# A split-precision first layer whose rescaling pass is dropped: three recombined passes summed in PSUM, units one by one

## The chip, the cores and the metric

The kernel runs on one core of a Trainium2 chip. The metric is device time in microseconds (us); the kernel before takes 2204.26 us, the median of three runs (2204.12 to 2204.32). The engines are called by the profile's names: PE is TensorE (PEld its weight loads), DVE VectorE, ACT ScalarE, POOL GpSimd, SP SyncE.

## The reference

A causal convolution along the sequence, with softmaxed weights per head, and then a two-layer perceptron with a hardswish between the layers:

```
x: 8 x 4096 x 192      weight: 8 heads x 7 taps
w   = softmax(weight) over the taps
y[b, s, h, :] = sum over k of w[h, k] * x_padded[b, s + k, h, :]   # 6 zeros ahead of the sequence
h   = y (32768 x 192) @ w_in (192 x 2048)
g   = h * clip(h + 3, 0, 6) / 6
out = g @ w_out (2048 x 192)                                     # float32
```

## The kernel before

The 32768 tokens are cut into 32 blocks of 1024. In a block, tokens 0 to 511 have their 192 channels on partitions 0 to 63 (three thirds per partition) and tokens 512 to 1023 on partitions 64 to 127. So a first-layer matmul works on 64 rows and 512 tokens, and two of them, one per half of the partitions, run side by side.

Block 0 is done in a plain way (`out_direct`, L341), while the weights of the others are prepared. Blocks 1 to 31 each call `first_layer` and then `second_layer`, and everything around them is written out by hand: the program's order on each engine is the order of the calls.

**The first layer in three passes.** The product y @ w_in is wanted in full precision but computed in a faster matmul format (`F32R`), whose operands are rounded. So y and w_in are each split. Of y the kernel makes three parts (L1068 to L1085): high p (`high_of`, ACT, L476, a multiplication by `CUT`), low l = y - p (`split_low`, DVE, L1081) and mix (`split_mix`, DVE, L479). Of w_in it makes three once, in the start (`w_parts`, L484). A unit is one of 16 pieces of a block's hidden features: 8 with the halves of the partitions as they lie (`y_own`), then 8 with the halves swapped (`y_other`, made by six DMAs from POOL's queue, L266 and L267). A unit has a slot of two PSUM banks out of four slots, and goes like this:

- `begin(n)`: the HIGH pass and the LOW pass, each three thirds times two halves, six matmuls (L511), into one slot; then both banks are multiplied by 4097 in place, by ACT (L523, 128x1024). For the last unit of a block ACT does one bank (L526) and DVE the other (L527).
- `end(n)`: the MIX pass adds six more matmuls to the rescaled sums; then ACT's `relu` (L302) and DVE's `gate` (L306) make g from the slot, which is free after that.

The order is begin(0), begin(1), then for every n end(n) and begin(n + 2); close to the end of the block begin(15) comes ahead of end(13). Hence the unit's third pass stands behind nine other matmul pairs or so, while ACT rescales. Between the units stand `jobs`: the last sums and stores of the block before (`finish`), and one tap of the convolution of the block after the next (L1058, DVE, 128x1536) after every second unit. POOL makes small sums of g (L603) beside it.

**The second layer.** It is computed by a scheme with seven products of halves of g and w_out in place of eight, partly two levels deep, with four streams of matmuls side by side in column tiles of 32 (L653). `second_layer` writes the streams with a clock of 80 steps; `do(t, fn)` puts the work of the other engines at a time t of that clock, and the events are then issued sorted by time. `level_two` issues one product at the second level and copies its pieces out of PSUM at the clock of the matmuls plus `late_by`. `negative(pair)` (L572 on ACT, then an accumulating DMA from POOL's queue, L569) makes a piece of S3, which product 3 reads at the end. `split_high`, `split_low` and `split_mix` of the next block stand at the times 48.4, 57 and 70. In the last block (`last`) some of it stands in another order, for a shorter end.

Of the kernel before, what the change touches and what calls it, by code (L numbers as in the profile page):

```python
# [8 lines left out]
ALU = mybir.AluOpType  # L9
# [8 lines left out]


CUT = 1.0 - 2.0**-13  # L20
EPS = 2.0**-12
HIGH, LOW, MIX = range(3)


# [1 line left out]
def kernel(  # L26
# [8 lines left out]
    nc = tc.nc  # L35
# [11 lines left out]
    K3 = D // D2  # L47
# [424 lines left out]
    def r32(ap):  # L472
        return ap.bitcast(F32R)

    def high_of(out, x, scale=1.0):
        nc.scalar.mul(r32(out), x, CUT * scale)  # L476

    def from_high(out, high, scale, x, op):
        nc.vector.scalar_tensor_tensor(  # L479
            out=r32(out), in0=high, scalar=scale, in1=x, op0=ALU.mult, op1=op  # L480
        )
# [17 lines left out]
    def first_layer(i, jobs):  # L499

        slots = {}

        def both(n):
            return psum[:, 2 * slots[n] : 2 * slots[n] + 2]

        def mms(n, part, start=False, stop=False):
            group, c = divmod(n, NP)
            for s in range(K3):
                for k in range(2):
                    r = slice(k * D2, (k + 1) * D2)  # L510
                    nc.tensor.matmul(  # L511
                        out=psum[:, 2 * slots[n] + k], lhsT=r32(w_in_parts[part][r, c, s]),
                        rhs=r32(y_other[0][r, part, s] if group else y_own[part][r, s]),
                        start=start and s == 0, stop=stop and s == K3 - 1,
                        skip_group_check=True,
                    )

        def begin(n):
            slots[n] = free_slots.pop(0)
            mms(n, HIGH, start=True)  # L520
            mms(n, LOW)
            if n + 1 < count:
                nc.scalar.mul(both(n), both(n), 4097.0)  # L523
            else:
                lower, upper = (psum[:, 2 * slots[n] + k] for k in range(2))
                nc.scalar.mul(lower, lower, 4097.0)  # L526
                nc.vector.tensor_scalar(  # L527
                    out=upper, in0=upper, scalar1=4097.0, scalar2=None, op0=ALU.mult
                )
# [12 lines left out]
        for job in jobs.get(-1, ()):  # L542
            job()
        for n in range(count):
            if n == count - 3:
                begin(n + 2)
            end(n)
            if n < count - 3:
                begin(n + 2)
            for job in jobs.get(n, ()):  # L550
                job()
            if n < NP and n % 2:
                small_sums(shared, A11, (3, 2, 4), nc.gpsimd, every[n - 1 : n + 1])
            if n == NP - 1:
                sums4[:] = [pools[0].tile([P, NP, N], F32, name="z4", tag="own")]
                nc.sync.dma_start(out=four_parts(sums4[0])[0], in_=four_parts(A22)[2])
                small_sums(sums4[0], A22, (3,), nc.gpsimd, every[:4])
            if n == NP + 1:
                third_sum(0, nc.vector)
                add_pair(0)  # L560
                adding(four_parts(sums4[0])[0], four_parts(A22)[3])
                small_sums(sums4[0], A22, (3,), nc.gpsimd, every[4:])
            if n == NP + 3:
                third_sum(1)
                small_sums(sums4[0], A22, (2,), nc.gpsimd)
                add_pair(1)
# [54 lines left out]
    def second_layer(i, between):  # L621
# [118 lines left out]
        def level_two(n, p, order, j=3):  # L740
# [197 lines left out]
    with tc.manual_schedule():  # L938
# [129 lines left out]
        def split_y():  # L1068
            new_parts()
            high, low, mix = y_own  # L1070
            high_of(high[:], y[:])
            split_low()
            split_mix()

        def split_high():
            new_parts()
            high_of(y_own[HIGH][:], y[:])

        def split_low():
            high, low, mix = y_own  # L1080
# [87 lines left out]
```

## Time and profile before

| what | us |
|---|---|
| median of three runs | 2204.26 |
| the profiled execution | 2203.68 |
| its span (from the first to the last instruction) | 2201.9 |
| PE busy | 2193.5 |
| DVE busy | 1983.1 |
| ACT busy | 1738.8 |
| POOL busy | 1181.4 |
| a first layer on the chain that ended last | 32.97 |
| a second layer on that chain | 34.61 |
| rescaling on ACT (L523, 465 times 1008 ns) | 468.7 |

A row of a group gives line, engine, operation, output and inputs, partitions x elements and how many there were, then busy time in us and mean ns of one, then the engine's idle time just before them and what ended most of it. A row of the timeline gives start, duration and the same names; a note in square brackets is idle time of that engine ahead of the row, with what ended it. Several equal instructions that follow each other stand in one row (x24), whose duration runs from the first start to the last end. A row of the waits gives who waited for whom, the total in us, how often, and the longest. The granted TensorE clock is 0.999 of full speed over the span.

### The profile page before, as it was taken

How to read it: one execution, taken by the hardware profiler on the slowest of the kernel's cores; microseconds unless marked ns; L12 is line 12 of the kernel's file. 1: busy time of each engine (PE TensorE's matmuls, PEld its weight loads, DVE VectorE, ACT ScalarE, POOL GpSimd, SP SyncE). 2: the span in 40 equal slices, each digit the busy share in tenths (PEclk: the TensorE clock that was granted, in tenths of full speed). 3: DMA queues.
4: the chain of work that ended last, by engine and by line, in shares of the span. 5: the costliest groups of instructions: out<-in, count | busy, mean ns of one | idle time of the engine just before them, and what ended most of it. 6: DMA issues, size and time to landing. Idle time of an engine off the chain costs nothing.

```text
span 2201.9 us, 55361 instructions
## 1 busy us (share of the span) xinstructions
PE 2193.5 (100%) x22984; PEld 1564.6 (71%) x22984; DVE 1983.1 (90%) x1983; ACT 1738.8 (79%) x2391; POOL 1181.4 (54%) x1033
## 2 busy tenths in 40 slices
PE   9999999999999999999999999999999999999998
PEld 5477777777777777777777777777777777777776
DVE  8899998999898989989999999999899998999977
ACT  7488787787877878877878778787788887787876
POOL 2456644556544665445655456554456544556544
PEclk9999999999999999999999999999999999999999
DMA  6277778777778777797777887777877778777787
GB/s 158 56 141 142 144 148 154 139 144 145 146 140 159 139 140 143 146 163 131 144 146 146 149 148 141 145 144 144 159 134 141 145 148 155 136 145 143 134 142 121
DMA packets 353308, 313.20 MB, mean 142 GB/s; under 512 B 212480, under 2 KB 265216, under 8 KB 353056
## 3 DMA queue, kind: packets, MB, share of 16 engines
q0 software_dynamic: 114976, 234.46, 59.2%
q1 hardware_dynamic: 236840, 74.93, 16.9%
q8 instruction: 180, 2.95, 0.6%
q14 instruction: 72, 0.59, 0.1%
q10 hardware_dynamic: 1240, 0.27, 0.1%
HBM read 31.72 MB, written 25.17 MB: 26 GB/s over the span
## 4 chain that ended last, share of the span: by engine, by line
PE 99%; DVE 0%; DMA 0%; SPq 0%; ACT 0%; issue 0%; DVEq 0%; ACTq 0%
PE psum L653 49%; PE psum L511 46%; PE psum L296 2%; PE psum L341 2%; DMA x<-in_x_dram 0%; DVE shared L458 0%; SPq L100 0%; DVE shared L464 0%; SPq L133 0%; DVE top L175 0%; PE psum L953 0%; DVE y L255 0%; SPq L89 0%; ACT y L967 0%; ACT scale L186 0%
## 5 line engine op out<-in xcount | busy, mean ns | idle before, releaser
L653 PE MATMUL psum<-g,w_out 128*32 128x512 f32 (+1 forms) x5968 | 824.2, 503 | 0.0
L306 DVE SCALAR_TENSOR_TENSOR g<-g,psum 128x1024 f32<-128x1024 f32 (+1 forms) x528 | 619.2, 1186 | 108.3 <-ACT g L302 107.9
L653 PE MATMUL psum<-s,w_out 128*32 128x512 f32 (+1 forms) x3024 | 712.1, 585 | 0.0
L302 ACT ACTIVATE g<-psum,half 128x1024 f32<-128x1024 f32 (+1 forms) x528 | 565.2, 1087 | 5.9 <-PE psum L511 5.1
L653 PEld LDWEIGHTS psum<-g,w_out 128*32 128x32 f32 x5968 | 382.1, 110 | 221.9 <-issue 112.2
L511 PE MATMUL psum<-y_own,w_in 64*128 64x512 f32 x4464 | 523.3, 389 | 0.0
L511 PE MATMUL psum<-y_other,w_in 64*128 64x512 f32 x4464 | 516.0, 386 | 0.0
L523 ACT ACTIVATE psum<-psum 128x1024 f32<-128x1024 f32 x465 | 468.7, 1008 | 48.3 <-PE psum L511 46.2
L511 PEld LDWEIGHTS psum<-y_own,w_in 64*128 64x128 f32 x4464 | 413.5, 184 | 117.6 <-issue 26.0
L511 PEld LDWEIGHTS psum<-y_other,w_in 64*128 64x128 f32 x4464 | 418.1, 184 | 87.8
L603 POOL TENSOR_TENSOR shared<-g,shared 128x256 f32<-128x256 f32 x248 | 356.9, 1439 | 89.8 <-DVE g L306 58.1
L1058 DVE SCALAR_TENSOR_TENSOR y<-x,c_sb,y 128x1536 f32<-128x1536 f32 x186 | 335.2, 1802 | 1.5 <-ACT y L1056 1.3
L569 POOL DMA_DIRECT2D s<-g x124 | 148.4, 1197 | 293.5 <-ACT s L572 246.7
L653 PE MATMUL psum<-g,w_s 128*32 128x256 f32 x1488 | 284.5, 379 | 0.0
L653 PEld LDWEIGHTS psum<-s,w_out 128*32 128x32 f32 x3024 | 231.8, 110 | 34.5 <-issue 11.2
L569 POOL DMA_DIRECT2D g<-g x124 | 181.7, 1530 | 104.6 <-DVE s L414 104.6
L653 PE MATMUL psum<-z,w_s 128*32 128x256 f32 x992 | 227.7, 379 | 0.0
L653 PE MATMUL psum<-z,w_out 128*32 128x256 f32 x992 | 227.0, 379 | 0.0
L603 POOL TENSOR_TENSOR shared<-g 128x256 f32<-128x256 f32 x124 | 91.6, 739 | 174.1 <-DVE g L306 174.1
L650 ACT COPY psum<-psum 32x512 f32<-32x512 f32 x186 | 82.9, 446 | 116.1 <-PE psum L653 113.2
L458 DVE TENSOR_TENSOR g<-g 128x1024 f32<-128x1024 f32 x124 | 149.4, 1221 | 19.3 <-PE psum L653 17.1
L653 PEld LDWEIGHTS psum<-g,w_s 128*32 128x32 f32 x1488 | 137.8, 110 | 38.1
(115 smaller groups left out, 2870.1 us busy)
## 6 DMA issues: line engine op xcount, KB each, us to landing
y_other<-y_own POOLq DMA_DIRECT2D x180, 384.0 KB, 8.1
g<-g POOLq DMA_DIRECT2D x124, 512.0 KB, 6.1
s<-g POOLq DMA_DIRECT2D x124, 512.0 KB, 6.3
z<-g POOLq DMA_DIRECT2D x62, 512.0 KB, 7.5
out_dram<-shared SPq DMA_DIRECT2D x378, 64.0 KB, 4.3
x<-in_x_dram SPq DMA_DIRECT2D x53, 388.5 KB, 5.7
z<-g SPq DMA_DIRECT2D x31, 512.0 KB, 3.3
stage<-in_moe_w_in_dram SPq DMA_DIRECT2D x16, 192.0 KB, 4.6
```

Source lines behind the costliest of these rows:

```text
L296: nc.tensor.matmul(out=psum[:, b], lhsT=w[r], rhs=src, start=start, stop=stop, skip_group_check=onto,)
L302: nc.scalar.activation(r6, h, ACT.Relu, bias=half[:], scale=1.0 / 6.0)
L306: nc.vector.scalar_tensor_tensor(out=g_, in0=g_, scalar=1.0, in1=h, op0=ALU.min, op1=ALU.mult)
L341: lambda p=p: nc.tensor.matmul(out=bank[j * QS : (j + 1) * QS, tokens], lhsT=w_out[:, p, w, cols], rhs=x[:, p, tokens], start=(first and p ...
L458: nc.vector.tensor_tensor(out=out, in0=x, in1=y, op=op)
L511: nc.tensor.matmul(out=psum[:, 2 * slots[n] + k], lhsT=r32(w_in_parts[part][r, c, s]), rhs=r32(y_other[0][r, part, s] if group else y_own[ ...
L523: nc.scalar.mul(both(n), both(n), 4097.0)
L569: nc.gpsimd.dma_start(out=out, in_=x, accum_op=ALU.add)
L603: engine.tensor_tensor(out=o, in0=p, in1=q, op=op)
L650: streams[3].append((t - 0.5, lambda: fn(*args, **kw)))
L653: nc.tensor.matmul(out=out, lhsT=w, rhs=x, start=start, stop=True, tile_position=(0, j * QS), skip_group_check=True,)
L1058: jobs.append(lambda k=k: nc.vector.scalar_tensor_tensor(out=y[:], in0=x[:, :, k : k + N], scalar=c_sb[:, k : k + 1], in1=y[:], op0=ALU.mu ...
```

## The change

The three products are combined in another way. With y = p + l and w_in = H + L, where p and H are exact in the matmul format, the sum is now

p H + l (H + 4097 L) + (p - 4096 l) L,

in which the terms with 4096 and 4097 leave l L over: p H + l H + 4097 l L + p L - 4096 l L = (p + l)(H + L). Nothing has to be rescaled, so all 18 matmuls of a unit add to one another in PSUM. H is now w_in times 1 + 2^-13 in the rounded format. The parts stand in the order p with H, l with H + 4097 L, p - 4096 l with L, and the third part of y is -4096 l + p in place of p / 4096 - l.

A unit's 18 matmuls now stand together; unit n + 1's come ahead of the relu and gate of unit n. Two events of the last block's second layer are moved: the copy of product 4's second piece from 19.3 to 8.2 clock steps behind its matmuls, and the fourth `negative` from time 52 to 44.3. On the engines' queues this takes out 465 + 31 + 2 passes of ACT (L523, L526, L487) and 31 of DVE (L527) and moves one copy and one negation on ACT in the last block, its DMA with it; the order of POOL's and SP's instructions stays, and DVE's but for the passes taken out.

```diff
-EPS = 2.0**-12
+RAISE = 1.0 + 2.0**-13
...
-    def w_parts(high, low, mix, w):
-        high_of(high, w, EPS)
-        from_high(mix, high, 4097.0, w, ALU.subtract)
-        from_high(low, high, -4096.0, w, ALU.add)
-        nc.scalar.mul(r32(mix), mix, -4096.0)
+    def plus(out, x, scale, y):
+        nc.vector.scalar_tensor_tensor(
+            out=r32(out), in0=x, scalar=scale, in1=y, op0=ALU.mult, op1=ALU.add
+        )
+    def w_parts(high, sum_, low, w):
+        high_of(high, w, RAISE)
+        plus(low, high, -1.0, w)
+        plus(sum_, low, 4097.0, high)
...
-        def begin(n):
-            slots[n] = free_slots.pop(0)
-            mms(n, HIGH, start=True)
-            mms(n, LOW)
-            if n + 1 < count:
-                nc.scalar.mul(both(n), both(n), 4097.0)
-            else:
-                lower, upper = (psum[:, 2 * slots[n] + k] for k in range(2))
-                nc.scalar.mul(lower, lower, 4097.0)
-                nc.vector.tensor_scalar(
-                    out=upper, in0=upper, scalar1=4097.0, scalar2=None, op0=ALU.mult
-                )
         def end(n):
             group, c = divmod(n, NP)
-            mms(n, MIX, stop=True)
             to = g4[:, c, 1:3] if group else g4[:, c, 0::3]
             relu(to, both(n))
             gate(to, both(n))
             free_slots.append(slots[n])
-        begin(0)
-        begin(1)
+        steps = [(part, s) for part in range(3) for s in range(K3)]
+        mms(0)
         for job in jobs.get(-1, ()):
             job()
         for n in range(count):
-            if n == count - 3:
-                begin(n + 2)
+            if n + 1 < count:
+                mms(n + 1)
             end(n)
-            if n < count - 3:
-                begin(n + 2)
...
-                    late_by = {(1, 2): 8.1, (4, 2): 19.3}.get((n, k), 0.02 if n == 4 else 0)
+                    late_by = {(1, 2): 8.1, (4, 2): 8.2 if last else 19.3}.get((n, k), 0.02 if n == 4 else 0)
...
-        for r, t in zip(chunk_pairs, (34.3, 36.3, 42.1, 52)):
+        for r, t in zip(chunk_pairs, (34.3, 36.3, 42.1, 44.3 if last else 52)):
             do(t, negative, r)
...
         def split_mix():
             high, low, mix = y_own
-            from_high(mix[:], high[:], EPS, low[:], ALU.subtract)
+            plus(mix[:], low[:], -4096.0, high[:])
```

More of the change, by code (lines that the diff above doesn't have):

```diff
@@ L473, in r32, with high_of @@
         return ap.bitcast(F32R)
-    def high_of(out, x, scale=1.0):
-        nc.scalar.mul(r32(out), x, CUT * scale)
-    def from_high(out, high, scale, x, op):
+    def high_of(out, x, by):
+        nc.scalar.mul(r32(out), x, by)
+    def plus(out, x, scale, y):
         nc.vector.scalar_tensor_tensor(
-            out=r32(out), in0=high, scalar=scale, in1=x, op0=ALU.mult, op1=op
+            out=r32(out), in0=x, scalar=scale, in1=y, op0=ALU.mult, op1=ALU.add
         )
-    def w_parts(high, low, mix, w):
-        high_of(high, w, EPS)
-        from_high(mix, high, 4097.0, w, ALU.subtract)
-        from_high(low, high, -4096.0, w, ALU.add)
-        nc.scalar.mul(r32(mix), mix, -4096.0)
+    def w_parts(high, sum_, low, w):
+        high_of(high, w, RAISE)
+        plus(low, high, -1.0, w)
+        plus(sum_, low, 4097.0, high)
     free_slots = list(range(4))
@@ L504, in both, with mms @@
             return psum[:, 2 * slots[n] : 2 * slots[n] + 2]
-        def mms(n, part, start=False, stop=False):
+        def mms(n):
+            slots[n] = free_slots.pop(0)
             group, c = divmod(n, NP)
-            for s in range(K3):
+            for part, s in steps:
                 for k in range(2):
@@ L513, in mms @@
                         rhs=r32(y_other[0][r, part, s] if group else y_own[part][r, s]),
-                        start=start and s == 0, stop=stop and s == K3 - 1,
+                        start=(part, s) == steps[0], stop=(part, s) == steps[-1],
                         skip_group_check=True,
                     )
-        def begin(n):
-            slots[n] = free_slots.pop(0)
-            mms(n, HIGH, start=True)
-            mms(n, LOW)
-            if n + 1 < count:
-                nc.scalar.mul(both(n), both(n), 4097.0)
-            else:
-                lower, upper = (psum[:, 2 * slots[n] + k] for k in range(2))
-                nc.scalar.mul(lower, lower, 4097.0)
-                nc.vector.tensor_scalar(
-                    out=upper, in0=upper, scalar1=4097.0, scalar2=None, op0=ALU.mult
-                )
         def end(n):
             group, c = divmod(n, NP)
-            mms(n, MIX, stop=True)
             to = g4[:, c, 1:3] if group else g4[:, c, 0::3]
@@ L1070, in split_y @@
             high, low, mix = y_own
-            high_of(high[:], y[:])
+            high_of(high[:], y[:], CUT)
             split_low()
@@ L1076, in split_high @@
             new_parts()
-            high_of(y_own[HIGH][:], y[:])
+            high_of(y_own[HIGH][:], y[:], CUT)
         def split_low():
```

## The prediction

> **What bounds the kernel now.** I read the page's head first, then the chain that ended last in order of time, then TensorE's own waits, then the timelines of one block (the one whose first layer starts at 978.3 us; the blocks repeat to 0.01 us).
>
> ```profile
> span 2201.9 us, 55361 instructions
> PE 2193.5 (100%) x22984; PEld 1564.6 (71%) x22984; DVE 1983.1 (90%) x1983; ACT 1738.8 (79%) x2391; POOL 1181.4 (54%) x1033
> ```
> ```profile
> 943.79 34.61 PE psum L653 x289
> 978.40 32.97 PE psum L511 x288
> ```
> The chain is TensorE throughout: 31 times a first layer (L511, 288 matmuls, 32.97 us), then a second layer (L653, 34.61 us). The change edits the first layer, so what can be gained is what its 32.97 us hold beyond matmuls. All durations come from one profiled execution. ScalarE looks like the bound there, and a table of busy time by stage, from the third unit on, seems to say so:
>
> ```profile
> 981.40:1009.00 27.60, 27.60 (x246) 22.77 (x246) 25.61 (x20) 27.52 (x27) 19.95 (x17) 1.00 0.67 141
> ```
> Columns: stretch, length, then PE, PEld, DVE, ACT, POOL. ACT is busy 27.52 of 27.60 us, but PE all 27.60. Who waits for whom decides:
>
> ```profile
> PEld psum L511 <- issue: 26.0, 31, 0.8
> PEld psum L511 <- ACT psum L523: 6.8, 30, 0.2
> ```
> TensorE's weight loads wait for the rescaling (L523) once per block, 30 times, 6.8 us in all. That is load idle, not lost time; the matmul rows give the loss. Two matmuls, one per half of the rows, start together; I call them a pair.
>
> ```profile
> L511 PE MATMUL psum<-y_other,w_in 64*128 64x512 f32 x4464 | 516.0, 386 | 0.0
> ```
> ```profile
> 978.33 3.02 PE L511 MATMUL psum<-y_own,w_in 64*128 64x512 f32 x24
> ...
> 980.73 13.64 PE L511 MATMUL psum<-y_own,w_in 64*128 64x512 f32 x118
> 994.21 1.52 PE L511 MATMUL psum<-y_other,w_in 64*128 64x512 f32 x12
> ...
> 996.25 15.12 PE L511 MATMUL psum<-y_other,w_in 64*128 64x512 f32 x132
> ```
> The last row is 66 pairs, so 65 spacings in 15.12 - 0.386 us: 0.2267 us each, and 144 of them are 32.64 us. The 12 pairs from 978.33 take 3.02 - 0.386 - 11 x 0.2267 = 0.14 us too long: the start of the stage. The 59 pairs from 980.73 take 13.64 - 0.386 - 58 x 0.2267 = 0.11 us too long: the wait, at the first unit's third pass. The remaining 0.08 of 32.97 is the hand-over to the second layer.
>
> **The change part by part.**
>
> *The rescaling goes.*
>
> ```profile
> L306 DVE SCALAR_TENSOR_TENSOR g<-g,psum 128x1024 f32<-128x1024 f32 x496 | 598.8, 1218 | 106.5 <-ACT g L302 106.3
> L302 ACT ACTIVATE g<-psum,half 128x1024 f32<-128x1024 f32 x496 | 545.7, 1114 | 5.9 <-PE psum L511 5.1
> L523 ACT ACTIVATE psum<-psum 128x1024 f32<-128x1024 f32 x465 | 468.7, 1008 | 48.3 <-PE psum L511 46.2
> ...
> L527 DVE TENSOR_SCALAR psum<-psum 128x512 f32<-128x512 f32 x31 | 21.7, 700 | 4.3
> ```
> 465 x 1.008 = 469 us leave ScalarE and 22 us VectorE (and 31 half-size passes at L526, two at L487 in the start). All but the 30 waits lie beside matmuls, so they count nothing. The matmuls stay 288 per block at the same shapes. What goes is 30 x 0.11 = **3.2 us**. The lower bound is the first such block, the only one without the wait:
>
> ```profile
> 99.83 16.00 PE L511 MATMUL psum<-y_own,w_in 64*128 64x512 f32 x138
> ```
> Its 69 pairs take 16.00 - 0.386 - 68 x 0.2267 = 0.20 us too long, with no wait, against 0.14 + 0.11 = 0.25 elsewhere. If the other blocks settle as slowly once the wait is gone, only 0.05 x 30 = 1.4 us come back. I take 0.105 x 30 = 3.1, since their start has settled after 0.14 before the wait comes; above, 3.2.
>
> *Units one by one.* The first unit's third pass moves from pair 12 to pair 6 (counted from 0), so the third part of y (split_mix, L479) is needed earlier; its place in VectorE's queue stays.
>
> ```profile
> 976.14 1.71 DVE L479 SCALAR_TENSOR_TENSOR y_own<-y_own 128x1536 fp32r<-128x1536 f32 x1
> ...
> 981.87 1.77 DVE L1058 SCALAR_TENSOR_TENSOR y<-x,c_sb,y 128x1536 f32<-128x1536 f32 x1
> 983.57 1.22 DVE L306 SCALAR_TENSOR_TENSOR g<-g,psum 128x1024 f32<-128x1024 f32 x1
> ```
> It ends at 977.85; pair 6 starts at 978.33 + 0.14 + 6 x 0.2267 = 979.83, and its weight load, which waits, about one pair sooner: 1.75 us of cover. Behind that load all matmuls would queue. The swapped copy's third part is needed at pair 78 (996.2) instead of 84:
>
> ```profile
> 978.65 0.52 POOL L267 DMA_DIRECT2D y_other<-y_own  x1
> ```
> ```profile
> y_other<-y_own POOLq DMA_DIRECT2D x180, 384.0 KB, 8.1
> ```
> It lands about 978.65 + 8.1 = 986.8, 9 us ahead. A PSUM slot now returns four units later: unit 4 starts at pair 36 (986.6) and waits for the first gate, which VectorE reaches only behind the previous block's last sums and a convolution tap: 983.57 + 1.22 = 984.8, 1.8 us of cover. Gates then cost two times 1.22 and a tap 1.77 per two units, 4.2 us by single durations, but they overlap:
>
> ```profile
> 988.47 2.44 DVE L306 SCALAR_TENSOR_TENSOR g<-g,psum 128x1024 f32<-128x1024 f32 x2
> ...
> 992.55 2.44 DVE L306 SCALAR_TENSOR_TENSOR g<-g,psum 128x1024 f32<-128x1024 f32 x2
> ```
> 4.08 us from 988.47 to 992.55, which is 18 pairs x 0.2267: VectorE keeps step, and its cover stays. At the end only unit 15's gate is left after the last matmul instead of three, so the second layer's sums begin earlier. I count zero for all of this. Its first matmul now carries a wait, for unit 12's gate, done three units before; between nothing and what the start of the stage pays (0.14 us x 31 = 4.3), I take zero, since waits that are met cost nothing in the steady rows. The queues of SP and POOL keep their order and every DMA.
>
> The start: the new weight parts need one ScalarE pass less per half, beside block 0's matmuls, which the first layer follows without a break (99.83 above); zero.
>
> *Two moves in the last block.* TensorE stops twice there.
>
> ```profile
> 2177.37 0.38 PE L653 MATMUL psum<-g,w_out 128*32 128x256 f32 x1
> ...
> 2177.59 0.38 PE L653 MATMUL psum<-g,w_out 128*32 128x256 f32 x1
> ...
> 2178.37 0.41 PE L653 MATMUL psum<-g,w_out 128*32 128x256 f32 x2
> ...
> 2179.30 0.60 PE L653 MATMUL psum<-g,w_out 128*32 128x512 f32 x3
> ```
> ```profile
> 2178.37 0.11 PEld L653 LDWEIGHTS psum<-g,w_out 128*32 128x32 f32 x2 [0.82 <-ACT shared L744]
> ...
> 2191.34 0.12 PEld L653 LDWEIGHTS psum<-s,w_out 128*32 128x32 f32 x3 [0.32 <-DMA s<-g]
> ```
> ```profile
> 2177.97 0.35 ACT L744 COPY shared<-psum 32x256 f32<-32x256 f32 x1
> 2178.34 0.59 ACT L650 COPY psum<-z 96x512 f32<-96x512 f32 x1
> ...
> 2184.14 1.06 ACT L572 ACTIVATE s<-g 128x1024 f32<-128x1024 f32 x1
> ```
> Matmuls of 256 columns follow each other by 0.22 us, so 2178.37 is 0.56 late; the copy at 2177.97 is the one moved forward (product 4's second piece). But the copy behind it (L650, to 2178.93, of the first product into b) releases the matmul that starts at 2179.30 now and would start at 2178.74; everything ahead of L650 on ScalarE keeps its sum, so L650 doesn't come earlier, and 0.2 us are late next. Gain 0.3 of 0.56. The second stop:
>
> ```profile
> 2190.66 0.38 PE L653 MATMUL psum<-s,w_out 128*32 128x256 f32 x2
> ...
> 2191.34 0.42 PE L653 MATMUL psum<-s,w_out 128*32 128x256 f32 x3
> ```
> ```profile
> 2180.78 1.22 DVE L458 TENSOR_TENSOR g<-g 128x1024 f32<-128x1024 f32 x1
> ```
> 0.68 - 0.22 = 0.46 us, for the fourth negation's DMA. Its ScalarE part now stands right behind the small copies after 2181.2 instead of at 2184.14; it then waits for the sum that it reads, 2180.78 + 1.22 = 2182.0, or 0.4 later because the moved copy delays what is behind it. So it starts by 2182.4, 1.7 us sooner, and the stop goes. What comes after the last matmul moves along. Together **0.8 us**, between 0.3 (the second stop stays) and 1.0.
>
> **Sum.** 3.1 + 0.8 = 3.9 us. The profiled execution took 2203.68 us, 1.8 around its span; it would take 2199.8. The median of the runs, 2204.26, lies 0.58 above it: **2200.4**. Own range: gains from 1.4 + 0.3 to 3.2 + 1.0, so 2200.1 to 2202.6.
>
> A rule on the start of the stage: the Trainium skill, TensorEngine Tiling (Array Packing), Tiling Modes, says that a change of tiling mode drains TensorE. The rows agree in sign (0.14 at the start; two tiles of 64 rows follow four of 32 columns), and both kernels switch alike. By that rule the 0.14 stay and the sum is 3.9; without it they could go as in the first rival.
>
> **The rivals.**
>
> *More than the wait goes.* If the 0.14 at the start came from ScalarE or VectorE too, 30 x 0.25 + 0.20 + 1.0 = 8.7 us go: 2195.6. For it: the loads idle 0.84 us there. Against: the profile names no releaser for that idle ("issue"), and the first block pays it as well. Parts of it are enough to pass 4.4.
>
> *The spacing shrinks.* ScalarE's pace per unit is 2.04 us (L523 to L523), the same as 9 pairs; perhaps its PSUM passes set the 0.2267.
>
> ```profile
> 983.53 1.01 ACT L523 ACTIVATE psum<-psum 128x1024 f32<-128x1024 f32 x1
> ...
> 985.57 1.01 ACT L523 ACTIVATE psum<-psum 128x1024 f32<-128x1024 f32 x1
> ```
> ```profile
> 1013.49 0.59 PE L653 MATMUL psum<-s,w_out 128*32 128x512 f32 x1
> ...
> 1013.92 0.59 PE L653 MATMUL psum<-s,w_out 128*32 128x512 f32 x1
> ```
> In the second layer the rows of 512 columns follow by 0.43 us; if that is two passes, one is 0.215 (an estimate). At that spacing 144 x 31 x 0.012 = 53 us go: 2151. Against: the stage's weight loads show no wait but the one. The Trainium skill, TensorE: Matmul & The Clock Gate, Back-to-back issue gap, gives N/2.4 + 2.5 ns, 215.8 for 512 columns; our 226.7 differs, and by that rule 144 x 31 x 0.0109 = 49 us would be someone's stall.
>
> *It doesn't do what it says.* The wait at pair 12 turns into one of the same size at pair 6 or at a slot: 0 to 0.8 us gain, 2203.5 to 2204.3.
>
> *The third part of y comes late (slower).* Pair 6 waits in VectorE's queue for split_mix. Up to 1.75 us of delay nothing happens; each us beyond costs 30 us. If the sums of the previous block (977.85 to 981.87) came to stand ahead of it, it would end about 4.0 us later, 2.2 us too late: 30 x 2.2 = 66 - 4 = 62 us slower, 2266; at 0.5 us too late still 2215. For it: VectorE works without a break there. Against: its order of work is the same but for the 31 passes removed, and it hangs on the same matmuls.
>
> **How the numbers follow.** Forecast 0.72; more goes 0.14; spacing 0.02; nothing 0.05; third part late 0.07. A measurement of this kernel tells about 0.2% (4.4 us, so 2199.85) from no change. Faster by more: 0.14 + 0.02 = 0.16; within: 0.72 + 0.05 = 0.77; slower: 0.07. The range takes the forecast's own, the nearer half of "more goes" (down to 2198.8) and the nearest of "nothing": 2198.8 to 2203.6, about 0.81.
>
> **What would show it.** In the profile after: no L523-like group; ACT at least 469 us less busy; first layers of 32.86 in the chain, second layers still 34.61; no wait of TensorE's loads for ScalarE in the first layer; 0.14 at its start as before; in the last block no wait for the s<-g DMA and one of 0.2 for the copy into b. Wrong if a row "PEld psum <- DVE" appears about 30 times (third part, or a slot), if the matmul spacing isn't 0.2267, or if second layers grow.

## The result and the profile after

The changed kernel takes **2201.14 us** (median of 22 runs, 2200.67 to 2201.56) beside 2204.24 of the kernel before (22 runs, 2204.03 to 2204.78): a ratio of 0.9986, 95% interval 0.9979 to 0.9992. It is 3.1 us faster: no run of the one overlaps the runs of the other, though 0.14% are less than the 0.2% from which the prediction counts a change as faster. The profiled execution took 2200.85 us. The forecast was 2200.4, from 3.1 us in the first layers and 0.8 in the last block. The first layers gave 3.4; the last block gave nothing.

The head of the page: ScalarE is 450 us less busy, VectorE 30, and TensorE still has no room.

```profile
span 2199.1 us, 54306 instructions
PE 2190.2 (100%) x22984; PEld 1566.3 (71%) x22984; DVE 1953.6 (89%) x1952; ACT 1288.5 (59%) x1893; POOL 1182.4 (54%) x1033
```

The chain that ended last, its last pieces (start, length, what):

```profile
2089.36 34.61 PE psum L637 x289
2123.97 32.86 PE psum L511 x288
2156.83 12.27 PE psum L637 x116
...
2179.04 1.06 ACT s L556
2180.40 7.64 DMA s<-g
2188.08 1.11 PE psum L637 x16
```

Three things are to be seen. A first layer (L511) is 32.86 us long, 0.11 shorter than before. A second layer (now L637) still has 34.61. And the chain now leaves TensorE in the last block and runs through the fourth chunk's negation (L556) and its DMA, 7.64 us from issue to landing, which it did not do before.

TensorE's waiting weight loads in the first layers, over the whole run, and the two rows of matmuls of one first layer:

```profile
PEld psum L511 <- issue: 26.0, 31, 0.8
```
```profile
976.86 16.61 PE L511 MATMUL psum<-y_own,w_in 64*128 64x512 f32 x144
993.31 16.48 PE L511 MATMUL psum<-y_other,w_in 64*128 64x512 f32 x144
```

The row "PEld psum L511 <- ACT psum L523" is gone and no row with VectorE or ScalarE has taken its place. The second row is 72 pairs: 16.48 - 0.386 - 71 x 0.2267 = 0.00, nothing lost. The first: 16.61 - 0.386 - 16.10 = 0.13, the start of the stage, unchanged. Block 1, the first to run this stage, which before had 0.20 at this place, has 0.13 too.

The last block, its waits (those of the weight loads, and the one of a matmul itself):

```profile
PEld psum L637 <- DMA s<-g: 0.9, 1, 0.9
PEld psum L637 <- ACT psum L727: 0.4, 1, 0.4
PEld psum L637 <- ACT psum L634: 0.3, 1, 0.3
```
```profile
PE psum L637 <- DMA s<-g: 0.4, 1, 0.4
```

Before, there was 0.82 for the copy of product 4's second piece and 0.32 for the DMA. The first has gone, with two short waits in its place; the second has grown to 0.9. Why, the issues on GpSimd's queue of the four negations' DMAs show; before, then after:

```profile
2176.62 1.18 POOL L569 DMA_DIRECT2D s<-g  x1 [4.26 <-ACT s L572]
2178.36 1.20 POOL L569 DMA_DIRECT2D s<-g  x1 [0.57 <-ACT shared L744]
2181.06 1.21 POOL L569 DMA_DIRECT2D s<-g  x1 [1.50 <-ACT s L572]
2185.50 1.20 POOL L569 DMA_DIRECT2D s<-g  x1 [3.23 <-ACT s L572]
```
```profile
2173.62 1.18 POOL L553 DMA_DIRECT2D s<-g  x1 [5.09 <-ACT s L556]
2175.36 1.20 POOL L553 DMA_DIRECT2D s<-g  x1 [0.57 <-ACT s L556]
2177.81 1.21 POOL L553 DMA_DIRECT2D s<-g  x1 [1.24 <-ACT s L556]
2180.40 1.20 POOL L553 DMA_DIRECT2D s<-g  x1 [1.38 <-ACT s L556]
```

The last second layer starts 3.40 us earlier than before (2160.16 to 2156.76, its first matmul). Counted from there, the first DMA is issued at 16.46 before and 16.86 after, 0.40 later, because the moved copy (0.37) stands ahead of its negation; the fourth at 25.34 and 23.64, 1.70 sooner, as forecast. It lands at 31.14 before and at 31.27 after (its last completion comes at 2188.03): 0.13 **later**. From 0.9 us behind the first issue to the last landing the DMA engines are full (stretch, length, the five engines' busy times, granted clock, DMA share, GB/s; before, then after):

```profile
2177.50:2191.30 13.80, 13.80 (x186) 7.93 (x177) 10.18 (x15) 8.82 (x18) 3.90 (x4) 1.00 0.97 164
```
```profile
2174.50:2188.00 13.50, 13.18 (x179) 8.67 (x171) 10.68 (x16) 8.56 (x17) 3.90 (x4) 1.00 1.01 169
```

13.8 us at 164 GB/s are 2.26 MB, 13.5 at 169 are 2.28: the same bytes in the same time, four chunks of 512 KB and some stores. An earlier issue of the fourth joins a queue.

So the spans come out: 3.40 gained up to the last second layer, 0.13 lost in it (its last matmul starts at 35.46 instead of 35.33), and 0.44 lost behind it, where the last sums and stores end 6.85 us after that matmul's start instead of 6.41. 3.40 - 0.13 - 0.44 = 2.8, which is 2201.9 - 2199.1.

### The profile page after: what moved, and what is told of

The parts are those of the page before. It is cut to its first block, busy times and chain, and to the rows that moved or that the text cites. A ratio compares the mean times of both kernels' runs of the same rounds, so it can differ in the third digit from the quotient of the medians.

```text
span 2199.1 us, 54306 instructions
## 1 busy us (share of the span) xinstructions
PE 2190.2 (100%) x22984; PEld 1566.3 (71%) x22984; DVE 1953.6 (89%) x1952; ACT 1288.5 (59%) x1893; POOL 1182.4 (54%) x1033
## 4 chain that ended last, share of the span: by engine, by line
PE 98%; DMA 1%; DVE 0%; ACT 0%; issue 0%; SPq 0%; DVEq 0%; ACTq 0%
PE psum L637 48%; PE psum L511 46%; PE psum L296 2%; PE psum L341 2%; DMA s<-g 0%; DMA x<-in_x_dram 0%; DVE shared L458 0%; ACT s L556 0%; SPq L100 0%; DVE g L587 0%; DVE g L458 0%; DVE shared L464 0%; SPq L133 0%; DVE top L175 0%; PE psum L937 0%
## 5 line engine op out<-in xcount | busy, mean ns | idle before, releaser
L302 ACT ACTIVATE g<-psum,half 128x1024 f32<-128x1024 f32 (+1 forms) x528 | 574.4, 1092 | 487.4 <-PE psum L511 460.7
L637 PE MATMUL psum<-g,w_out 128*32 128x512 f32 (+1 forms) x5968 | 824.2, 503 | 0.0
L637 PE MATMUL psum<-s,w_out 128*32 128x512 f32 (+1 forms) x3024 | 711.6, 585 | 0.4 <-DMA s<-g 0.4
L306 DVE SCALAR_TENSOR_TENSOR g<-g,psum 128x1024 f32<-128x1024 f32 (+1 forms) x528 | 608.4, 1181 | 108.4 <-ACT g L302 108.1
L637 PEld LDWEIGHTS psum<-g,w_out 128*32 128x32 f32 x5968 | 382.5, 110 | 221.2 <-issue 112.4
L511 PE MATMUL psum<-y_own,w_in 64*128 64x512 f32 x4464 | 515.0, 388 | 0.0
L511 PE MATMUL psum<-y_other,w_in 64*128 64x512 f32 x4464 | 510.9, 386 | 0.0
L511 PEld LDWEIGHTS psum<-y_own,w_in 64*128 64x128 f32 x4464 | 415.8, 184 | 112.1 <-issue 26.0
L511 PEld LDWEIGHTS psum<-y_other,w_in 64*128 64x128 f32 x4464 | 418.1, 184 | 87.8
L637 PE MATMUL psum<-g,w_s 128*32 128x256 f32 x1488 | 284.6, 379 | 0.0
L637 PEld LDWEIGHTS psum<-s,w_out 128*32 128x32 f32 x3024 | 231.6, 110 | 34.7 <-issue 11.2
L637 PE MATMUL psum<-z,w_s 128*32 128x256 f32 x992 | 227.5, 379 | 0.0
L637 PE MATMUL psum<-z,w_out 128*32 128x256 f32 x992 | 227.0, 379 | 0.0
L637 PEld LDWEIGHTS psum<-g,w_s 128*32 128x32 f32 x1488 | 137.8, 110 | 38.3 <-ACT psum L727 0.4
L553 POOL DMA_DIRECT2D z<-g x62 | 96.2, 1551 | 117.7 <-ACT z L556 117.7
```

What stands on the lines that cost most here:

```text
L302: nc.scalar.activation(r6, h, ACT.Relu, bias=half[:], scale=1.0 / 6.0)
L306: nc.vector.scalar_tensor_tensor(out=g_, in0=g_, scalar=1.0, in1=h, op0=ALU.min, op1=ALU.mult)
L511: nc.tensor.matmul(out=psum[:, 2 * slots[n] + k], lhsT=r32(w_in_parts[part][r, c, s]), rhs=r32(y_other[0][r, part, s] if group else y_own[ ...
L553: nc.gpsimd.dma_start(out=out, in_=x, accum_op=ALU.add)
L637: nc.tensor.matmul(out=out, lhsT=w, rhs=x, start=start, stop=True, tile_position=(0, j * QS), skip_group_check=True,)
```

## The experiments

Each kernel's time is the median of its own runs (11; 4 or 5 of the three slowest); the kernel before had 2204.11 to 2204.17 beside them. For the last block one number is used throughout: TensorE's **lag**, the start of a matmul, less the start of the last second layer, less the columns already issued (four tiles side by side, 512 columns in 0.427 us each). It is near zero while nothing stops TensorE, and swings by about 0.1 from one of the four tiles to the next. The columns give it at so many us of work. Stop A is the wait for product 4's second piece (after 17.4 us of work), stop B that for the fourth chunk (after 29.8). "Lands" is the last of the fourth DMA's 16 completions in the trace.

| kernel | lag at 16.5 | at 17.9 | at 29.5 | at 30.5 | at 34 | fourth chunk lands | last matmul | time, us |
|---|---|---|---|---|---|---|---|---|
| before | -0.02 | 0.72 | 0.80 | 1.21 | 1.25 | 31.14 | 35.33 | 2204.24 |
| changed | -0.05 | 0.15 | 0.39 | 1.34 | 1.38 | 31.27 | 35.46 | 2201.14 |
| neither move | -0.05 | 0.71 | 0.79 | 1.15 | 1.20 | 30.99 | 35.28 | 2200.80 |
| negation only | -0.05 | 0.71 | 0.79 | 1.16 | 1.21 | 31.10 | 35.29 | 2200.76 |
| copy behind first negation | -0.05 | 0.15 | 0.38 | 1.15 | 1.20 | 31.09 | 35.28 | 2200.81 |
| negations earlier | 0.07 | 0.33 | 1.18 | 1.10 | 1.74 | 30.33 | 35.82 | 2201.37 |
| fourth on GpSimd | -0.05 | 0.15 | 0.39 | 0.37 | 0.77 | no DMA | 34.85 | 2199.89 |

**Two theories for the first layers.** Mine: TensorE lost only what its load waited for at pair 12. The rival: ScalarE's 465 passes over PSUM, or the order of passes, slowed the matmuls by themselves. The next five kernels tell them apart.

*ScalarE's load put back without the wait.*

```
+            if n + 1 < count:
+                nc.scalar.mul(both(n), both(n), 1.0)
             relu(to, both(n))
             gate(to, both(n))
```

> The changed kernel with an idle pass put back on ScalarE: after each unit but the last is summed, its two banks are multiplied by 1.0 in place ahead of relu, the same instruction and size as the 465 rescalings that were taken out, but with no matmul of the unit behind it. Theory that only the wait at pair 12 cost time: within 0.3 us of the changed kernel (2201.1), ScalarE about 465 us busier, first layers still 32.86. Rival, that ScalarE's passes over PSUM slow the matmuls beside them: 1 to 3 us slower (2202 to 2204). If a PSUM slot comes back too late behind the longer tail, a wait of TensorE for VectorE or ScalarE shows at unit 4 or later and the time rises by its length times 31.

Measured: 2200.58 us (2200.25 to 2200.90), ratio to before 0.9984 [0.9975, 0.9993]. The page's head and a piece of the chain:

```profile
PE 2190.2 (100%) x22984; PEld 1567.0 (71%) x22984; DVE 1962.3 (89%) x1952; ACT 1712.2 (78%) x2358; POOL 1179.8 (54%) x1033
```
```profile
976.83 32.86 PE psum L511 x288
```

ScalarE is back at 78%, 465 instructions more, and the first layer keeps its 32.86. The rival falls: as many passes on ScalarE as before, beside the matmuls, cost TensorE nothing in the first layer. The time is 0.56 us below the changed kernel's, outside the 0.3 that I had put down; in its profile the stretch behind the last matmul's start, which scatters in this study, is 6.25 us instead of 6.85.

*The wait taken away, the rescaling kept.* In the kernel before, matmuls of the third unit were put ahead of the first unit's third pass: all six pairs of its first two passes, then three, one and two.

First all six (then m pairs of its first pass, further below):

```
         begin(0)
         begin(1)
+        begin(2)
...
-            if n < count - 3:
+            if 0 < n < count - 3:
                 begin(n + 2)
```

> The kernel before, with every rescaling, and with one thing changed: the third unit's first two passes stand ahead of the first unit's third pass, so the third pass comes at pair 18 instead of pair 12 and finds its rescaling done. Theory that the gain in the first layer is TensorE's wait at pair 12 and nothing else: 30 x 0.107 = 3.2 us faster than before (2201.0 where before has 2204.2), first layers of 32.86 us with ScalarE as busy as before. Rival, that the gain comes from ScalarE's and VectorE's lighter load in PSUM or from the order of passes: no more than 0.3 us faster, first layers of 32.97.

Measured: 2213.48 us, ratio 1.0043 [1.0030, 1.0055], 9.3 us slower. Missed by both theories:

```profile
PEld psum L511 <- DVE g L306: 16.2, 31, 0.5
```

The wait at pair 12 is gone, and a longer one has come at pair 33: the first unit's PSUM slot comes back too late for the fifth unit, since relu and gate start six pairs later. That loses 0.41 us per block, of which the wait at pair 12 gives back 0.11. So fewer pairs, with m = 3, 1 and 2, and the rest of `begin(2)` where it was:

```
+            if n == 0:
+                slots[2] = free_slots.pop(0)
+                mms(2, HIGH, start=True, chunks=range(m))
             end(n)
```

> The kernel before, with every rescaling, and one thing changed: three pairs (the third unit's first pass) stand ahead of the first unit's third pass, which so comes at pair 15 instead of 12. Its PSUM slots come back 0.7 us sooner than in the kernel that put all six pairs there, which ran into a new wait of 0.4 for VectorE's gate at pair 33 in every block. Theory that the gain in the first layer is the wait at pair 12 and nothing else: 30 x 0.107 = 3.2 us faster than before (2200.9 where before has 2204.1), first layers of 32.86 with ScalarE as busy as before. Rival, that the lighter load on ScalarE or the order of units gave it: no change (2204.1).

Measured: 2205.62 us (2204.99 to 2206.09), ratio 1.0006 [0.9997, 1.0015].

```profile
PEld psum L511 <- DVE g L306: 7.9, 30, 0.3
```

A miss again, with m = 3: no wait at pair 12 and none at 33, but one of 0.26 us of the load at pair 51, for a gate. First layers are 33.02. What such a wait costs is instructive: pair 51 itself starts on time, within 4 ns, and the gap behind it is 109 ns too long, then 9, 6 and 4. This is the sequence that stands at the start of every first layer (110, 9, 5, 4), and 0.13 in sum. At pair 12 of the kernel before it is much the same, with 80 in front. Where a load waits for so short a time, its own matmul is not late; the loss is the restart, the spacings behind it.

> The kernel before, with every rescaling, and one pair of the third unit put ahead of the first unit's third pass, which so comes at pair 13 instead of 12. (With three pairs there, the wait at pair 12 was gone but the weight load at pair 51 waited 0.26 us for VectorE's gate, at the same loss.) Theory that a waiting weight load costs about 0.11 us and ScalarE's load nothing: one pair is 0.227 us, as long as the load's wait at pair 12, so that wait is nearly or wholly gone and the later one does not arise: 2.0 to 3.2 us faster than before (2200.9 to 2202.1 where before has 2204.1), first layers of 32.86 to 32.90, ScalarE as busy as before. Rival, that the gain hangs on ScalarE's or VectorE's lighter load: 2204.1.

> The same with two pairs ahead, the third pass at pair 14. Same theory: the wait at pair 12 is gone for certain, the later one for the gate is 0.04 us long if it arises at all; 2.0 to 3.3 us faster than before if it does not (2200.8 to 2202.1), no gain if even so short a wait of a load costs 0.11. Rival, that the gain hangs on ScalarE's or VectorE's lighter load: 2204.1.

Measured: 2201.01 us (2200.52 to 2201.39) with one pair, ratio 0.9985 [0.9977, 0.9994]; 2200.93 (2200.80 to 2201.24) with two, ratio 0.9986 [0.9977, 0.9995]. The head and a piece of the chain, with one pair:

```profile
PE 2191.1 (100%) x22984; PEld 1567.7 (71%) x22984; DVE 1982.0 (90%) x1983; ACT 1736.1 (79%) x2391; POOL 1181.7 (54%) x1033
```
```profile
977.11 32.86 PE psum L511 x288
```

All rescaling is there, ScalarE at 79% as before, no load in the first layers waits for ScalarE or VectorE, and the 3.2 us are won: one or two pairs moved do all that the recombined passes did for the time.

**What the 0.13 us at the stage's start are.** Four matmuls of the second layer's shape (tiles of 32 columns) were put into the first layer, ahead of the ninth unit.

```
+            if n == NP:
+                for j in range(4):
+                    nc.tensor.matmul(
+                        out=psum[rows(j), 2 * slots[n]], lhsT=w_out[:, 0, 0, 0:QS],
+                        rhs=y_own[HIGH][:, 0], start=True, stop=True,
+                        tile_position=(0, j * QS), skip_group_check=True)
```

> The changed kernel with four more matmuls per first layer, in tiles of 32 columns and 512 wide as in the second layer, at the start of the ninth unit; what they write is overwritten by that unit's first matmuls. It asks what the 0.13 us at the start of the first layer are. If a change between tiles of 32 columns and tiles of 64 rows costs a restart each time (0.13 us, the two changes added here cost 0.2 to 0.3), the time rises by 31 x (0.43 + 0.2 to 0.3) = 20 to 23 us, to 2221 to 2224, and the pairs behind the extra matmuls show the row 110, 9, 5, 4 ns of the stage's start. If the change of tiles is free and the stage's start has another cause, by 31 x 0.43 = 13 us, to 2214.

Measured: 2239.09 us, ratio 1.0158 [1.0144, 1.0172]; against the changed kernel 37.95 us, 1.22 per first layer, more than either theory gave. TensorE's rows:

```profile
992.95 16.61 PE L518 MATMUL psum<-y_own,w_in 64*128 64x512 f32 x144
1009.50 1.06 PE L509 MATMUL psum<-y_own,w_out 128*32 128x512 f32 x8
1010.49 16.62 PE L518 MATMUL psum<-y_other,w_in 64*128 64x512 f32 x144
```

The four matmuls are 8 records, two for each; four side by side take 0.43 us, so all take 0.86 and not the 0.43 that I had put down. The remaining 0.36 are the two changes: the hand-over into the extra matmuls, 1009.50 - 992.95 - 0.13 - 72 x 0.2267 = 0.10; the one out of them, 1010.49 - 1009.50 - 0.86 = 0.13; and again the restart, 16.62 - 0.386 - 16.10 = 0.14, in a row that loses nothing in the changed kernel (16.48). So the change costs the restart in the middle of a stage as at its start. The Trainium skill, TensorEngine Tiling (Array Packing), Tiling Modes, says that a change of mode drains TensorE; the trace agrees in that each change costs time, 0.10 us in one direction and 0.27 in the other. One thing is not separated: the extra matmuls, like the second layer's, also have plain float32 operands where the first layer's are `F32R`, so that tiles and number format change together, and no run here changes one alone.

**The third part of y made late.** The split of the third part, and its swap, were put behind the previous block's last sums; in the program the first unit's matmuls stand behind those sums too, so that they read the new part.

```
-                between += [(48.4, split_high), (57, split_low), (70, split_mix)]
+                between += [(48.4, split_high), (57, split_low)]
...
             left = second_layer(i, between)
+            if i + 1 < NB:
+                left += [split_mix, lambda: swap_parts(nc.gpsimd, (MIX,))]
```

> The changed kernel with the third part of y split behind the previous block's last sums instead of ahead of them (and its swap and the tile's order with it): the prediction's slower rival, made on purpose. The prediction's price: the third part comes 2.2 us too late for pair 6 and 30 x 2.2 = 66 us are lost, 2267. Refined from the changed kernel's trace, where those sums cannot start sooner since they wait for the second layer's last matmuls: split at 980.4 to 982.1 in the block whose first layer starts at 976.9, pair 6's load due at 978.2, 3.9 late, 30 x 3.9 = 117 us: 2318. If the order of the third part did not matter (the cover is longer than read): 2201.

Measured: 2379.16 us (2378.91 to 2379.41), ratio 1.0794 [1.0779, 1.0808]: 178 us more than the changed kernel, 5.93 for each of the 30 blocks.

```profile
PEld psum L511 <- DVE y_own L479: 122.0, 30, 4.1
```
```profile
975.23 1.33 PE L511 MATMUL psum<-y_own,w_in 64*128 64x512 f32 x10
980.19 10.02 PE L511 MATMUL psum<-y_own,w_in 64*128 64x512 f32 x64 [3.63 <-DVE y_own L479]
```
```profile
976.50:980.00 3.50, 0.06 (x2) 0.00 (x0) 3.43 (x4) 0.00 (x0) 0.00 (x0) 0.81 1.02 250
980.00:981.00 1.00, 0.81 (x4) 0.71 (x6) 1.00 (x2) 0.00 (x0) 0.57 (x2) 0.50 1.13 258
...
984.00:985.00 1.00, 1.00 (x6) 0.76 (x6) 0.25 (x1) 0.00 (x0) 0.66 (x1) 0.50 1.03 236
985.00:986.00 1.00, 1.00 (x10) 0.76 (x8) 0.00 (x0) 0.29 (x1) 0.06 (x1) 0.74 1.02 223
986.00:1000.00 14.00, 14.00 (x126) 12.00 (x124) 13.12 (x10) 7.53 (x7) 10.78 (x9) 1.00 0.10 16
```

The pair that needs the third part was due at 975.23 + 1.33 - 0.386 + 0.2267 = 976.40 and starts 3.79 us late, as refined from the trace (3.9), not 2.2. The rest, 2.1 us, is something that the price left out: in the third view the granted clock (the column behind the five engines) is 0.50 from 980 to past 985, and the pairs of those microseconds follow each other by 0.427 us instead of 0.227. After a stop of 3.6 us the clock is at one half for some 7 pairs (3 us) in one block and some 12 (5 us) in the next, by turns. The Trainium skill, TensorE: Matmul & The Clock Gate, Part 1, What's actually happening, states that the clock is at one half after at least one idle window of about 3.4 us, until about 3.4 us of work have passed, and that the window runs freely. The trace agrees in the lengths: the clock stays at one half for 3.41 us or for 6.83, one such window or two. It does not agree that a whole window must be idle: 0.81 over the 3.5 us from 976.5 means one half from about 978.7 on, 2.1 us after the end of TensorE's last matmul (976.56); in the next block it is 3.3 us. The other stops of this study, 0.1 to 1 us long, left the mean granted clock at 0.999 or 1.00.

**Two theories for the last block.** The prediction's: ScalarE's order sets when the fourth chunk lands. The rival, from the trace after: the four DMAs' bytes do, and the moved copy delays the first of them.

*Without the moves, and with one of them.* In the first kernel both constants are those of before (19.3 for product 4's second piece, 52 for the fourth negation), in the second only the 19.3; in the third the copy is due at 14.4, behind the first negation.

> The changed kernel without the two moves in the last block (product 4's second piece and the fourth negation stand where they stood before). Compared with the changed kernel's 2201.1 us. Theory of the accumulating DMAs: the moves are worth nothing, because the fourth chunk of S3 lands when the four DMAs' bytes have gone through, and the moved copy delays the first of them by 0.4 us; so this kernel stays within 0.3 us of 2201.1, its first wait (0.55 us, for the copy of product 4's piece) is back, and the last chunk lands 0.1 us earlier, counted from the last second layer's start, than with the moves. The prediction's theory: the moves save 0.8 us, so this kernel takes 2201.9.

> The changed kernel with only the fourth negation moved forward in the last block; product 4's second piece is copied where it was before. Theory of the accumulating DMAs: without the moved copy the first negation starts 0.4 us earlier and the fourth is issued early, so its chunk lands 0.3 to 0.5 us earlier than in the changed kernel, counted from the last second layer's start; TensorE's wait for it falls from about 0.9 to about 0.5, and the wait for product 4's piece (0.55) is back: within 0.3 us of 2201.1. The prediction's theory: the stop for the fourth chunk goes altogether (the landing 1.7 us earlier) and the time is 2201.4, 0.3 to 0.5 us better than without either move.

> The changed kernel with product 4's second piece copied behind the first negation of the last block instead of ahead of it (the fourth negation stays early). Compared with the kernel that has only the fourth negation moved, 2200.8 us, in which the stop for that piece is 0.6 and the fourth chunk's last packet lands 31.1 us after the last second layer's start. Theory of the accumulating DMAs: the first stop is as small as in the changed kernel, the chunks land as without the moved copy (last packet at 31.0 to 31.1), so TensorE still stops there, for 0.8 to 0.9, and the last matmul starts at 35.3: within 0.3 us of 2200.8. If ScalarE's order alone set the end (the prediction's theory), 0.5 us are gained: 2200.3.

Measured: 2200.80 us (2200.43 to 2201.16), 2200.76 (2200.60 to 2201.13) and 2200.81 (2200.59 to 2200.96). The prediction's theory had asked for 2201.9, 2201.4 and 2200.3: undoing the moves loses nothing, and the three kernels are alike. The fourth DMA's issue in the first and in the second of them, and TensorE's wait for it:

```profile
2182.12 1.20 POOL L553 DMA_DIRECT2D s<-g  x1 [3.23 <-ACT s L556]
```
```profile
PEld psum L637 <- DMA s<-g: 0.2, 1, 0.2
```
```profile
2179.96 1.20 POOL L553 DMA_DIRECT2D s<-g  x1 [1.13 <-ACT s L556]
```
```profile
PEld psum L637 <- DMA s<-g: 0.3, 1, 0.3
```

Issued 2.1 us sooner (25.3 to 23.2 after the second layer's start), the fourth chunk lands at 31.10 instead of 30.99. So between these two places the negation's order on ScalarE has no say in the landing. (I had expected 0.3 to 0.5 us sooner than in the changed kernel; it is 0.17.) One part I had not expected: of the fourth DMA's 16 completions the median comes 0.4 us sooner with the negation moved (29.90, without it 30.33), but the last stays at 31.1, and TensorE needs all 16. Why the last one trails the one before it by 0.3 to 1.3 us, in nearly all of these DMAs but the first of each row (under 0.1), is open. In the third kernel stop A is gone and the copy no longer delays the first negation, and still the last matmul starts at 35.28: what is won at stop A is waited for at stop B. The moved copy in front of the first negation costs the 0.17 us that the changed kernel has more (35.46). This is more than scatter: in the four profiles of this study with both moves the last matmul starts at 35.46 to 35.66, in the six with neither at 35.28 to 35.33. That the changed kernel's median is 0.3 us above these three agrees, but the runs overlap.

*The DMAs earlier, or one fewer.* First the negations of the first two chunks were issued earlier (30 and 33.5 instead of 34.3 and 36.3). Then, on the kernel with the copy behind the first negation, GpSimd, idle there, formed the fourth chunk by itself:

```
         def negative(pair):
+            if last and pair == chunk_pairs[3]:
+                nc.gpsimd.tensor_tensor(
+                    out=S3[:, pair], in0=A12[:, pair], in1=S2[:, pair], op=ALU.subtract)
+            else:
+                difference(S3[:, pair], A12[:, pair], S2[:, pair])
-            difference(S3[:, pair], A12[:, pair], S2[:, pair])
```

> The kernel with the copy behind the first negation, and the first two negations of the last block also issued earlier (due at 30 and 33.5 instead of 34.3 and 36.3), so that the row of the four accumulating DMAs starts 1 to 1.5 us sooner. Theory that the DMAs' bytes set the landing: every chunk lands 1 to 1.5 us sooner, the fourth's last packet at 29.6 to 30.1 after the second layer's start, TensorE's stop of 0.9 for it goes, the last matmul starts at 34.4 to 34.7 instead of 35.3 to 35.5, and the time is 2200.0 to 2200.4 (0.7 to 0.9 less than with no move). Rival, that the landing hangs on the fourth negation's own issue: it lands as before and nothing changes (2200.8).

> The kernel with product 4's second piece copied behind the first negation (2200.8 us), and the fourth chunk of S3 in the last block formed by one subtraction on GpSimd (128x1024, 3.4 us by the rows of that size, starting at about 12.5 us after VectorE has made its input, with no ScalarE pass and no DMA) instead of by ScalarE's negation and an accumulating DMA. Theory of the accumulating DMAs: the fourth chunk is ready some 5 us sooner, only three DMAs of 512 KB are left and the third lands no later than 27.5 to 28.5 us after the last second layer's start; TensorE's stop of 0.76 goes, its lag at the end falls from 1.20 to 0.4 or 0.5 us, and the time is 2200.0 to 2200.2. Rival, that another wait takes the stop's place (as with the negations issued earlier, where ScalarE's copies came late): 2200.6 to 2201.

Measured: 2201.37 us (2201.26 to 2201.66) and **2199.89** (2199.76 to 2200.25), ratio 0.9981 [0.9972, 0.9990]. With the negations earlier, and with GpSimd:

```profile
PEld psum L637 <- ACT psum L634: 0.9, 2, 0.5
PEld psum L637 <- ACT psum L727: 0.8, 1, 0.8
```
```profile
2179.44 3.22 POOL L699 TENSOR_TENSOR s<-g 128x1024 f32<-128x1024 f32 x1
```
```profile
PEld psum L637 <- ACT psum L732: 0.4, 1, 0.4
PEld psum L637 <- ACT psum L634: 0.3, 1, 0.3
```

With the negations earlier the first DMA is issued 0.9 us sooner than with the copy behind the first negation, all four chunks land 0.8 to 1.7 us sooner, the fourth at 30.33, and no load waits for it. The fourth itself is issued 1.0 us later (24.61 instead of 23.62 after the second layer's start), and still lands 0.8 sooner: the bytes ahead of it set the landing, not its own issue. Its issue with the copy behind the first negation, and with the negations earlier:

```profile
2180.61 1.20 POOL L553 DMA_DIRECT2D s<-g  x1 [1.38 <-ACT s L556]
```
```profile
2181.60 1.20 POOL L553 DMA_DIRECT2D s<-g  x1 [1.81 <-ACT s L556]
```

But ScalarE is one queue, the small copies behind the two negations came late (the waits above), and the lag was 1.1 ahead of stop B already. I had expected a gain; what went was the wait for the DMA, what came were three for ScalarE. With GpSimd the fourth chunk is ready at 2182.66, 25.6 us after the second layer's start, 5.5 sooner than by DMA. Stop B is gone, a wait of 0.4 us comes late in its place, and 0.9 us are won on the kernel that it was made from, 0.43 of them in the last matmul's start (34.85 instead of 35.28) and the rest behind it. The third DMA lands no sooner for it (28.56, 28.55 without). It is the only version whose runs all lie below those of both kernels.

## Why the prediction was right, and where it was wrong

- **The rescaling goes: right.** 30 x 0.107 = 3.2 us by first layers of 32.86 instead of 32.97, where 30 x 0.105 was taken. The reason held in both directions: load back without wait, nothing lost; wait gone with the load kept, all won. The lower bound of 1.4 (0.05 x 30 is 1.5), from the first such block, was not needed: that block's own 0.20 shrank to 0.13. With these 0.07 and a start of its first layer that is 0.12 us earlier (counted as zero) 3.40 were gained up to the last second layer.
- **Units one by one: right**, zero. No wait for a slot, the third part or the swapped copy came. That its order decides is shown by the kernel with the late third part, whose 178 us are 2.7 times the 66 of the rival's working: the sums that it waits for could not begin sooner (3.8 us late, not 2.2), and "each us beyond costs 30 us" stops holding where TensorE's idle time halves its clock.
- **Two moves in the last block: wrong.** The step that failed is "So it starts by 2182.4, 1.7 us sooner, and the stop goes." Its DMA was issued 1.7 us sooner, and the stop grew from 0.41 to 0.95 in lag. The working took the time from issue to landing as fixed. It was 5.80 us before and became 7.64: the DMA waits behind the three others, and an issue 1.70 sooner only waits longer. (The first of the four, with none of them ahead, takes 5.0 to 5.1.) Stop A's part was right (0.3 forecast, 0.41 less lag at 29.5 us of work) and was worth nothing, because stop B, which ends at a time that TensorE doesn't set, took it back. The 0.8 became -0.13 in the last matmul.
- **The sum:** 3.1 + 0.8 = 3.9 were forecast. The profiled execution has 3.40 - 0.13 up to the last matmul and loses 0.44 behind it; the medians have 3.1. That these equal the first term alone is in part luck. In the profiles of this study the time behind the last matmul's start is 6.2 to 7.1 us without an order that I can see; its cause stays open.
- **The rivals.** More than the wait goes: no, the 0.13 at the start stayed; it comes with the change of tiles (and of the number format), and the same sequence stands behind a load that came late for another reason. The spacing shrinks: no, 0.2267 in every kernel here at the full clock, with ScalarE at 59 or at 79%.
- **"ACT at least 469 us less busy"** was wrong by its arithmetic: it is 450, and the 465 passes put back added 424. Passes on ScalarE overlap, and busy time counts an overlap once; before, relu's pass begins at 984.45, where the rescaling of 983.53 lasts to 984.54:

```profile
984.45 1.11 ACT L302 ACTIVATE g<-psum,half 128x1024 f32<-128x1024 f32 x1
```

## What to carry to other kernels

Before work is taken off a busy engine, look for the one instruction of the bounding engine that waits for it: here 469 us of ScalarE's passes were worth 3.2 us, and moving one pair of matmuls ahead of the wait was worth the same. Where several DMAs are under way and the DMA share is near 1, price a transfer by the bytes ahead of it and not by the time from issue to landing; then it helps to start the whole row sooner or to take a transfer out of it, and an earlier issue of the last one does not. A gain ahead of a fixed deadline is no gain: ask first which stop comes last.

## What the runs showed of the hardware

- A weight load that waits 0.2 to 0.3 us costs TensorE 0.11 to 0.16 us even where the matmul behind it is on time: the gap behind the first pair is 80 or 109 ns too long and some of the next by 3 to 9.
- Changing from tiles of 64 rows (`F32R`) to tiles of 32 columns (float32) cost 0.10 us, and back 0.27.
- A stop of 3.6 us brought the granted clock to one half, as little as 2.1 us after the end of the last matmul, and some 3 or 5 us of work passed at that clock; so a pair that came 3.8 us late cost 5.9.
- Four accumulating DMAs of 512 KB between tiles of the on-chip memory, with some stores, kept all 16 engines full (share 0.97 to 1.01) at 164 to 169 GB/s; the last of a DMA's 16 completions mostly came 0.3 to 1.3 us behind the one before it.
